# Attention packed into 32 rows and a gated feed-forward: loads of k, q, v and p issued singly behind weight pieces, and the second batch's even sums of v ahead of its odd scores

## The chip, the cores and the metric

The kernel runs on one core of one Trainium2 chip. The metric is the device time of one execution in microseconds. Three runs were timed; a further execution was profiled, and all durations below come from that one.

## What is computed

Eight batches of eight heads attend twice. First 32 packing rows p attend to k and v of 576 rows; then q attends to the packed rows. The result, 4608 tokens of 512, goes through a gated feed-forward without a nonlinearity.

```python
def sm_attn(qq, kk, vv):
    s = scale * np.matmul(qq, kk.transpose(0, 1, 3, 2))
    a = np.exp(s - np.max(s, axis=-1, keepdims=True))
    a = a / (np.sum(a, axis=-1, keepdims=True) + 1e-09)
    return np.matmul(a, vv)
p_packed = sm_attn(p, k, v)
out = sm_attn(q, p_packed, p_packed)
x = out.transpose(0, 2, 1, 3).reshape(B * S, H * D)
return ((x @ w_a) * (x @ w_b)) @ w_out
```

## The kernel before, in words

Every matmul of the feed-forward is made of three: each operand is split into a rounded high part and a low part, and high x high, high x low and low x high are added in PSUM. The tiles hold heads in two halves, "even" and "odd" (e = 0, 1); the loads, the scores and the sums of v are made once for each.

**The work of a batch.** `stage1` (L268) makes the scores of p against k (L276), their maximum, the exponentials (L294), their transposition (L315, L316), and the sums of v (L325), which VectorE scales into `pp` (L331). `stage2` (L334) makes the scores of q against the packed rows (L340) and their softmax into `a2_hi` and `a2_lo`. `g_tiles` (L395) folds the packed rows into the weights w_a and w_b, `mm1` (L416) makes the two gated factors, VectorE multiplies them (L431), and `mm2_part` (L442) multiplies by w_out.

**The order is written by hand.** All five engines run their instructions in the order in which the program issues them. Strings of steps set that order: `START` for the beginning, and `PLAN_0`, one piece between two bars for each slot between the half products of batch 0. In them `S0`/`S1` are the even and odd scores of the next batch, `r0`/`r1` the further steps of the even and odd `stage1` (the fourth one after the scores makes the sums of v), `s0`/`s1` those of `stage2`, `k`, `q` and `T` transpose k, q and p on VectorE (`turn` L120, `turn_p` L245), and `A B C D` convert a piece of the weights. `Lk`, `Lq`, `Lv`, `Lp` load k, q, v and p.

**Loads.** All loads that matter here are issued on SyncE's queue. A weight piece (`raw`, 512 KB, L224 and L231) is loaded as soon as a converted one leaves its buffer (`load_pieces`); 24 of them make w_a and w_b, 12 make w_out. `load` (L107) brings one half of k or q in four DMAs of 144 KB each, in packets of 128 bytes; `load_p` brings p in four of 32 KB, `load_v` a half of v in two of 256 KB and two of 32 KB. Each of these sends its DMAs at once, so that k or q goes out as a burst of four. A DMA also waits until the one eight places ahead of it has landed, because eight semaphores go round. `nat0` and `nat1` take k and then q; `vt` holds one half of v, so that the odd half can be loaded only when the even sums have read the even one.

**Banks.** PSUM tiles come from three pools. `m` has two bank pairs, which the half products of `mm1` and, behind them, the four output tiles of `mm2_part` take in turn (tiles 0 and 2 in one pair, 1 and 3 in the other). `s` is a single bank pair: the scores, the transposed exponentials and the sums of v of a later batch all go through it.

Of the kernel before, what the change touches and what calls it, by code (L numbers as in the profile page):

```python
# [19 lines left out]
def tile_packed_attn_gated_ffn(  # L20
# [20 lines left out]
    nc = tc.nc  # L41
    B, H, S, D = q.shape
    J = p.shape[2]
    DM, DF = w_a.shape
    DO = out.shape[1]
    P = 128
    R, E = 4, 2
# [3 lines left out]
    TL = 32  # L51
    TX = S // TL
    XH = TX // 2
    TR = HS - 2 * P
# [48 lines left out]


    nats, xTs = {}, {}

    def load(src, key, b, i):  # L107


        t = ld.tile([P, R, XH, TL], F32, name=f"nat{i}")  # L110
        rows = src[b, R * i:R * i + R].rearrange("h s d -> (h s) d")
        rows = rows.rearrange("(y l u) d -> u l y d" if key == "k" else "(y u l) d -> u l y d", u=2, l=TL)
        for u in range(2):
            for w in range(2):
                g = 64 * u + 32 * w
                nc.sync.dma_start(
                    out=t[g:g + TL].rearrange("l h x d -> l (h x) d"), in_=rows[u][:, :, TL * w:TL * w + TL])
        nats[key, b, i] = t

    def turn(key, b, i):  # L120
# [43 lines left out]
    def load_v(b, e):  # L164


        t = ld.tile([P, R, NT, D], F32, name="vt") if b or e == 0 else scratch.tile([P, R, NT, D], F32, name="vt1")
        vv = v[b].rearrange("(r e) s d -> e s r d", e=E)[e]
        n = 2 if b else 4
        for i in range(4 // n):  # L170
            nc.sync.dma_start(
                out=t[:, :, n * i:n * i + n, :].rearrange("p r u d -> p r (u d)"),
                in_=vv[n * P * i:n * P * i + n * P].rearrange("(p u) r d -> p r u d", u=n).rearrange("p r u d -> p r (u d)"))
        for u in range(2):
            nc.sync.dma_start(
                out=t[TR * u:TR * u + TR, :, 4, :],
                in_=vv[4 * P:S].rearrange("(p u) r d -> u p r d", u=2)[u])
        vts[b, e] = t

    def load_p(b, queue=None):  # L180
        if b:
            t = sm.tile([P, H, TL], F32, name="p_nat", bufs=1)
            halves = p[b].rearrange("h j (g d) -> g j h d", g=2)
            for g in range(4):
                nc.sync.dma_start(out=t[J * g:J * g + J], in_=halves[g % 2])
        else:
            t = sm.tile([P, 2, 2, D], F32, name="p_nat", bufs=1)
            rows = p[b].rearrange("h j d -> (h j) d").rearrange("(p c) d -> p c d", c=2)
            x = scratch.tile([P, 2, D], F32, name="p_in")
            queue.dma_start(out=x.rearrange("p c d -> p (c d)"), in_=rows.rearrange("p c d -> p (c d)"))  # L190
            nc.vector.tensor_copy(out=t, in_=x.unsqueeze(2).broadcast_to([P, 2, 2, D]))
        p_nat[b] = t
# [36 lines left out]
    def load_wout(f):  # L229
        raw = wop.tile([P, DO, 2], U32, name="raw", tag="w")  # L230
        nc.sync.dma_start(  # L231
            out=raw, in_=w_out.bitcast(U32)[P * f:P * f + P, :].rearrange("p (n t) -> p n t", t=2))
        raws[NC, f] = raw
# [248 lines left out]
    def emit(b, plan, tasks={}):  # L482

        for name in plan.split():
            if name in tasks:
                next(tasks[name], None)
                continue
            if name == "Z":
                warm_first()
                continue  # L490
            if name in "Ww":
                warm(9 if name == "W" else 1)
                continue
            if name in "ABCD":
                convert(name)
                continue
            what, e = name[:-1], int(name[-1])
            n = b + (e // 2 if b or what[0] == "L" else 0)
            if n >= B:
                continue  # L500
            if what == "S":
                if e == 0:
                    st[b] = [stage1(b, 0), stage1(b, 1), stage2(b, 0), stage2(b, 1)]
                next(st[b][e])
            elif what == "s":
                next(st[b][2 + e], None)
            elif what == "r":
                next(st[b][e], None)
            elif what == "T":
                turn_p(n)  # L510
            elif what == "P":
                turned(ppT[:, b % 2:b % 2 + 2], pp.pop(b), b % 2)
            elif what in ("k", "q"):
                turn(what, n, e % 2) if b else turn_first(what, e)
            elif what == "Lk":
                load(k, "k", n, e % 2)
            elif what == "Lq":
                load(q, "q", n, e % 2)
            elif what == "Lv":
                load_v(n, e % 2)  # L520
            elif what == "Lp":
                load_p(n)

    st = {}

# [2 lines left out]
    def warm_first():  # L528

        x = bank_pair()[:, 0, :]  # L530
        nc.tensor.matmul(out=x[:, 0:2 * P], lhsT=zero[:, 0:P], rhs=zero, start=True, stop=True)

    FIRST = ("k0 P0 K1 k2 q0 q1 v0 q2 v1 w1 w1 w1 w1 w1 w1 w1 w1 w1 w1 w1")
    START = ("Z Z Z Z T0 k0 k1 k2 k4 k3 q0 S0 S1 r0 r1 q1 q2 r1 r0 r0 r1 q4 r0 r1 q3 P0 s0 s1 B W A s0 B A A B s0 A s0 C B s1 C s1 s0 B C s1 A s1 B C Lp2 A A B s0 g s1 s0 g w s1 g C B B B C A Lk2 A C A B C A A B B Lk3 C C")
    WAYS = ("000000021020002100012012011200010010")
    TURN = ("1101110010")
    SUBS = ("0000")
# [1 line left out]
    PLAN = (" |  |  | S0 | r0 | r0 |  | r0 |  | r0 Lv1 ; S1 | r1 | r1 q0 Lk2 | r1 | r1 | q1 Lk3 Lv2 P0 |  ; s0 | s0 s0 | s0 T2 | "  # L539
            "s0 Lp4 | s0 s1 | s1 s1 | s1 | s1 | s1 | t0 t1 t2 t3 u0 | k2 |  | k3 Lq2")  # L540
    PLAN = dict(enumerate(PLAN.split("|")))
    PLAN_0 = ("A | C C | B A B A | B C C B C | A A | C | B Lv0 | C B A T0 k0 Lp2 | A A B C Lq0 | C k1 | A B A B A C | S0 B | B A r0 | C C C B A Lq1 | | | C C B r0 r0 D A A | S1 C D | B C B B A D | r1 C | A A D | r0 T2 | | q0 B r1 C B D r1 C | | A D B | C Lv1 A r1 A B D | Lk2 B C B q1 D Lk3 A A P0 | C s0 s0 D C Lp4 A B | s1 s0 | Lv2 | D | s0 s1 s0 | k2 s0 s1 C k3 | s1 | | Lq2 D s0 s1 s1 Lq3 s1")
    PLAN_0 = dict(enumerate(PLAN_0.split("|")))

    pieces = [(c, n) for c in range(NC) for n in range(4)] + [(NC, f) for f in range(NFT)]
    unloaded, to_do = list(pieces), {x: list(pieces) for x in "ABC"}

    def load_pieces(n):

        for _ in range(n):  # L550
            if unloaded and len(raws) + len(wo_hi) + len(wo_f32) < NFT:
                c, r = unloaded.pop(0)
                if c < NC:
                    load_w(c, r)
                else:
                    load_wout(r)

    def convert(x):

        if x == "D":  # L560
            if wo_f32:
                split_wout(wo_f32.pop(0))
                load_pieces(2)
            return
        if not to_do[x]:
            return
        c, n = to_do[x].pop(0)
        if (c, n) not in raws:
            load_pieces(1)
        raw = raws[c, n]  # L570
        if x == "A":
            high_word(raw)
        elif x == "B":
            low_word(raw, int(WAYS[pieces.index((c, n))]))
        else:
            assert len(to_do["A"]) <= len(to_do[x]) and len(to_do["B"]) <= len(to_do[x])
            if c < NC:
                i, rr = divmod(n, 2)
                both_words(w_ab[:, c, 2 * rr:2 * rr + 2, 2 * P * i:2 * P * i + 2 * P], raw)
            else:  # L580
                t = sm.tile([P, DO], F32, name="wo_f32", bufs=1)
                both_words(t, raw)
                wo_f32.append(t)
            del raws[c, n]
            load_pieces(2)

    def warm(n):

        x = bank_pair()[:, 0, :]
        t = firsts["k", 0].rearrange("p h t -> p (h t)")  # L590
        for _ in range(n):
            nc.tensor.matmul(out=x, lhsT=ident, rhs=t[:, 0:512], start=True, stop=True)
# [17 lines left out]
    for name in FIRST.split():  # L610
        what, i = name[0].lower(), int(name[1])
        queue = nc.sync if what == name[0] else nc.scalar
        if what == "p":
            load_p(0, queue)
        elif what == "v":
            load_v(0, i)
        elif what == "w":
            load_pieces(i)
        else:
            load_first(k if what == "k" else q, what, i, queue)  # L620
    tasks = {"g": next_g(0)}
    emit(0, START, tasks)
    drain(tasks["g"])
# [53 lines left out]
    for b in range(NB):  # L677
        plan = dict(PLAN if b else PLAN_0)
        slot, tasks, late_steps = [0], {"g": next_g(b + 1)} if b == 0 else {}, [""]
# [280 lines left out]
    i, c0 = tiles[-1]  # L960
# [35 lines left out]
```

## Time and profile before

| | us |
|---|---|
| median of three runs | 709.51 |
| lowest and highest run | 708.51, 713.61 |
| the profiled execution | 712.88 |
| span of its trace, first to last instruction | 711.1 |
| mean granted TensorE clock, share of full | 0.997 |
| TensorE matmuls busy | 699.6 (98%) |
| VectorE, ScalarE, GpSimd busy | 449.5, 364.7, 410.7 |

Times inside the trace count from the start of the span. The profiled execution lies 3.4 us above the median of the runs. A busy TensorE is not TensorE at its peak, since matmuls overlap and their ends are modelled; what its timeline shows reliably is when it stood and for whom. In a row of a timeline the bracket at the end gives the idle time just before it and what ended it. "SPq" is SyncE's queue, on which a row is the time that the issue of a DMA took, and "DMA" in the chain of waits is a transfer from its issue to its landing.

### The profile page before, as it was taken

How to read it: one execution, taken by the hardware profiler on the slowest of the kernel's cores; microseconds unless marked ns; L12 is line 12 of the kernel's file. 1: busy time of each engine (PE TensorE's matmuls, PEld its weight loads, DVE VectorE, ACT ScalarE, POOL GpSimd, SP SyncE). 2: the span in 40 equal slices, each digit the busy share in tenths (PEclk: the TensorE clock that was granted, in tenths of full speed). 3: DMA queues.
4: the chain of work that ended last, by engine and by line, in shares of the span. 5: the costliest groups of instructions: out<-in, count | busy, mean ns of one | idle time of the engine just before them, and what ended most of it. 6: DMA issues, size and time to landing. Idle time of an engine off the chain costs nothing.

```text
span 711.1 us, 14173 instructions
## 1 busy us (share of the span) xinstructions
PE 699.6 (98%) x5542; PEld 574.8 (81%) x5542; DVE 449.5 (63%) x825; ACT 364.7 (51%) x731; POOL 410.7 (58%) x320
## 2 busy tenths in 40 slices
PE   8999989999999999999999999999999999999998
PEld 6487867888778887887888788788788888888886
DVE  4988645367355669665875678765785667754342
ACT  5988734454344455644563456554555445544510
POOL 0556633337334787745874579566775577856520
PEclk9999999999999999999999999999999999999999
DMA  9999962668344745556444573456246323133002
GB/s 311 378 212 321 244 127 62 184 152 289 90 96 141 217 93 144 136 138 148 136 105 125 143 191 94 108 177 168 72 103 176 105 90 120 60 118 119 1 1 74
DMA packets 180371, 102.57 MB, mean 144 GB/s; under 512 B 145744, under 2 KB 161744, under 8 KB 174928
## 3 DMA queue, kind: packets, MB, share of 16 engines
q1 hardware_dynamic: 179888, 101.08, 50.8%
q8 instruction: 43, 0.70, 0.4%
q10 hardware_dynamic: 416, 0.59, 0.2%
q14 instruction: 24, 0.20, 0.1%
HBM read 85.92 MB, written 15.73 MB: 143 GB/s over the span
## 4 chain that ended last, share of the span: by engine, by line
PE 89%; DMA 7%; DVE 1%; ACT 1%; SPq 1%; issue 1%; DVEq 0%; ACTq 0%
PE x L764 37%; PE m L805 29%; PE m L416 8%; PE x L819 5%; PE m L442 4%; DMA raw<-in_moe_w_a_dram 2%; DMA vt<-in_v_dram 2%; PE s L325 2%; DMA raw<-in_moe_w_out_dram 1%; PE s L340 1%; PE s L276 1%; PE x L395 1%; PE s L315 1%; DMA wr<-w_kept 1%; DMA nat<-in_k_dram 1%
## 5 line engine op out<-in xcount | busy, mean ns | idle before, releaser
L764 PE MATMUL x<-wo,h_hi 128*128 128x512 f32 (+1 forms) x776 | 249.3, 391 | 0.3 <-ACT gs L825 0.3
L91 POOL TENSOR_TENSOR h_lo<-asb,h_hi 128x576 fp32r<-128x576 f32 x96 | 140.0, 1460 | 89.2 <-ACT h_hi L435 45.1
L764 PEld LDWEIGHTS x<-wo,h_hi 128*128 128x128 f32 x776 | 140.8, 188 | 22.4 <-ACT gs L825 1.3
L764 PE MATMUL x<-wo,h_lo 128*128 128x512 f32 (+1 forms) x388 | 152.0, 392 | 0.0
L91 POOL TENSOR_TENSOR G_lo<-gs,G_hi 128x640 fp32r<-128x640 f32 x72 | 112.9, 1573 | 30.9 <-ACT G_hi L840 30.6
L764 PEld LDWEIGHTS x<-wo,h_lo 128*128 128x128 f32 x388 | 72.9, 188 | 11.7
L91 POOL TENSOR_TENSOR A_lo<-gs,A_hi 128x256 fp32r<-128x256 f32 x36 | 27.2, 755 | 89.3 <-ACT A_hi L828 89.3
L887 DVE TENSOR_TENSOR d<-m,d 128x576 f32<-128x576 f32 (+1 forms) x73 | 54.1, 741 | 34.9 <-ACT d L883 34.1
L900 DVE TENSOR_TENSOR asb<-m,d 128x288 f32<-128x288 f32 x72 | 32.5, 451 | 64.1 <-ACT c L896 60.7
L896 ACT COPY c<-m 128x288 f32<-128x288 f32 x72 | 28.7, 399 | 83.2 <-PE m L805 83.2
L774 DVE TENSOR_TENSOR part<-x,part 128x512 f32<-128x512 f32 (+1 forms) x65 | 44.1, 678 | 38.7 <-PE x L764 38.7
L805 PE MATMUL m<-tx_hi,G_hi 128*128 128x288 f32 x216 | 63.8, 295 | 0.0
L805 PE MATMUL m<-tx_hi,G_lo 128*128 128x288 f32 x216 | 63.7, 295 | 0.0
L825 ACT COPY gs<-x 128x512 f32<-128x512 f32 x36 | 21.1, 587 | 83.0 <-PE x L819 81.4
L805 PE MATMUL m<-tx_lo,G_hi 128*128 128x288 f32 x216 | 63.3, 293 | 0.0
L840 ACT CAST G_hi<-gs 128x640 fp32r<-128x640 f32 x72 | 52.2, 729 | 15.1 <-POOL gs L834 14.5
L883 ACT COPY d<-m 128x576 f32<-128x576 f32 (+1 forms) x73 | 46.7, 639 | 20.1 <-PE m L805 18.5
L850 ACT CAST h_hi<-asb 128x576 fp32r<-128x576 f32 x72 | 49.0, 680 | 11.5 <-DVE asb L914 11.5
L805 PEld LDWEIGHTS m<-a_hi,G_hi 128*128 128x128 f32 x144 | 27.0, 187 | 31.8 <-issue 17.4
L834 POOL TENSOR_TENSOR gs<-gs 128x512 f32<-128x512 f32 x36 | 46.6, 1295 | 2.6 <-DVE gs L831 2.5
L805 PE MATMUL m<-a_hi,G_hi 128*128 128x288 f32 x144 | 46.6, 324 | 0.0
L913 DVE TENSOR_TENSOR m<-m,c 128x288 f32<-128x288 f32 x72 | 33.3, 463 | 17.7 <-PE m L805 16.0
(168 smaller groups left out, 1553.5 us busy)
## 6 DMA issues: line engine op xcount, KB each, us to landing
wr<-w_kept SPq DMA_DIRECT2D x36, 1024.0 KB, 5.1
nat<-in_k_dram SPq DMA_DIRECT2D x56, 144.0 KB, 5.3
nat<-in_q_dram SPq DMA_DIRECT2D x56, 144.0 KB, 5.3
vt<-in_v_dram SPq DMA_DIRECT2D x28, 256.0 KB, 3.6
out_dram<-part SPq DMA_DIRECT2D x27, 256.0 KB, 2.0
raw<-in_moe_w_a_dram SPq DMA_DIRECT2D x12, 512.0 KB, 8.4
raw<-in_moe_w_b_dram SPq DMA_DIRECT2D x12, 512.0 KB, 9.6
raw<-in_moe_w_out_dram SPq DMA_DIRECT2D x12, 512.0 KB, 6.9
```

The source lines that it names most:

```text
L91: return eng.tensor_tensor(out=dst, in0=src, in1=hi.bitcast(F32), op=ALU.subtract)
L416: nc.tensor.matmul(out=ps[:, half, 0:HS], lhsT=gt[:, kt, ft % 4, cols], rhs=at[:, kt, HS * half:HS * half + HS], start=(n == 0 and kt == 0 ...
L764: nc.tensor.matmul(out=o[:, cols], lhsT=ht[:, c0:c0 + P], rhs=wt[:, cols], start=(ft == fts[0] and n == 0), stop=end)
L774: nc.vector.tensor_tensor(out=parts[i][:, cols], in0=o[:, cols], in1=parts[i][:, cols], op=ALU.add)
L805: nc.tensor.matmul(out=bank[:, n % 2, 0:HS], lhsT=g, rhs=t, start=(first and i == 0), stop=(i == 2), skip_group_check=True)
L819: nc.tensor.matmul(out=gps[e][J * r:J * r + J, :], lhsT=ppT[rows, 2 * (b % 2), r, :], rhs=w[rows, r, :], start=True, stop=True)
L834: nc.gpsimd.tensor_tensor(out=gs[:, 2:4].rearrange("p a u f -> p a (u f)"), in0=gs[:, 0:2].rearrange("p a u f -> p a (u f)"), in1=s2.unsqu ...
L840: nc.scalar.copy(out=G_hi[:, n % 3], in_=gs[:, 1:6, n % 2])
L850: nc.scalar.copy(out=view(h_hi[ft]), in_=src)
L883: nc.scalar.copy(out=d[:, both], in_=X[:, both, 0:HS])
L887: nc.vector.tensor_tensor(out=d[:, both], in0=V[:, both, 0:HS], in1=d[:, both], op=ALU.add)
L913: nc.vector.tensor_tensor(out=v, in0=v, in1=c2, op=ALU.add)
```

## The change

Loads are no longer sent where they are asked for. `load`, `load_v` and `load_p` put their DMAs into a list, `parcels`, with a size, and `send` takes them from its front: after each weight piece as many as fit into 144 (a k or q piece counts 72, a p piece 16, half a v 32), and all of them once no weight piece is left to load. With the last weight piece loaded, each load is sent at once, as before.

```diff
+    parcels, unloaded = [], []
+    def parcel(size, out, in_):
+        parcels.append((size, out, in_))
+    def send(room=None):
+        while parcels and (room is None or parcels[0][0] <= room):
+            size, out, in_ = parcels.pop(0)
+            nc.sync.dma_start(out=out, in_=in_)
+            room = room and room - size
...
-                nc.sync.dma_start(
-                    out=t[g:g + TL].rearrange("l h x d -> l (h x) d"), in_=rows[u][:, :, TL * w:TL * w + TL])
+                parcel(2 * XH * R, t[g:g + TL].rearrange("l h x d -> l (h x) d"), rows[u][:, :, TL * w:TL * w + TL])
...
-                nc.sync.dma_start(out=t[J * g:J * g + J], in_=halves[g % 2])
+                parcel(2 * H, t[J * g:J * g + J], halves[g % 2])
...
+            if what[0] == "L" and not unloaded:
+                send()
...
+    ROOM = 144
...
                     load_wout(r)
+                send(ROOM)
+                if not unloaded:
+                    send()
...
         elif what == "v":
             load_v(0, i)
+            send()
```

Of the strings of steps, `START` asks for both halves of k of batch 1 directly behind `Lp2` instead of later. In `PLAN_0` the second half of q (`Lq1`) moves from slot 13 to slot 9, p of batch 2 (`Lp2`) from slot 7 to slot 11, the even sums of v (the last `r0`) from slot 21 to slot 17, ahead of `S1`, and the odd half of v (`Lv1`) from slot 26 to slot 17 behind them. `T2`, which transposes p of batch 2, stays in slot 21.

```diff
-    ... | S0 B | B A r0 | C C C B A Lq1 | | | C C B r0 r0 D A A | S1 C D | ... | r0 T2 | ... | C Lv1 A r1 A B D | ...
+    ... | S0 B Lp2 | B A r0 | C C C B A | | | C C B r0 r0 D A A | r0 Lv1 S1 C D | ... | T2 | ... | C A r1 A B D | ...
```

On SyncE's queue, from the last weight pieces of w_out on, the order before is this. `nat` with q is q of batch 1, the first `vt` its even half of v and the second its odd half, `p_nat` is p of batch 2.

```order
L171 DMA vt<-in_v_dram 128x4x128 x2
L175 DMA vt<-in_v_dram 32x4x64 x2
L231 DMA raw<-in_moe_w_out_dram 128x1024
L185 DMA p_nat<-in_p_dram 32x8x32 x4
L231 DMA raw<-in_moe_w_out_dram 128x1024
L116 DMA nat_731<-in_q_dram 32x36x32 x4
L231 DMA raw<-in_moe_w_out_dram 128x1024 x5
L116 DMA nat_874<-in_q_dram 32x36x32 x4
L231 DMA raw<-in_moe_w_out_dram 128x1024
L171 DMA vt<-in_v_dram 128x4x128 x2
L175 DMA vt<-in_v_dram 32x4x64 x2
```

The same place of SyncE's queue now (the lines of the changed kernel stand 9 to 17 further down; L116 is the `send` of all parcels, L240 the w_out piece):

```order
L116 DMA vt<-in_v_dram 128x4x128 x2
L116 DMA vt<-in_v_dram 32x4x64 x2
L240 DMA raw<-in_moe_w_out_dram 128x1024 x2
L116 DMA nat_726<-in_q_dram 32x36x32 x2
L240 DMA raw<-in_moe_w_out_dram 128x1024
L116 DMA nat_726<-in_q_dram 32x36x32 x2
L240 DMA raw<-in_moe_w_out_dram 128x1024
L116 DMA nat_750<-in_q_dram 32x36x32 x2
L240 DMA raw<-in_moe_w_out_dram 128x1024
L116 DMA nat_750<-in_q_dram 32x36x32 x2
L240 DMA raw<-in_moe_w_out_dram 128x1024
L116 DMA p_nat<-in_p_dram 32x8x32 x4
```

The q pieces stand in pairs between weight pieces, and p of batch 2 has moved from ahead of all q to behind it, directly ahead of the last weight piece and the odd half of v. One w_out piece more stands ahead of the even half of v. The k pieces of batch 1, further up, are taken apart in the same way, with one piece of w_a more ahead of their end.

On TensorE, at the odd scores of batch 1 (`xT` is transposed k, `pT` transposed p), before:

```order
L416 MATMUL m<-a_hi,glo 128x288 x4
L276 MATMUL s<-xT_703,pT 32x288 x2
L276 MATMUL s<-xT_755,pT 32x288 x2
L276 MATMUL s<-xT_703,pT 32x256 x2
L276 MATMUL s<-xT_755,pT 32x256 x2
```

And now:

```order
L425 MATMUL m<-a_hi,glo 128x288 x4
L334 MATMUL s<-vt,t_947 32x64 x20
L285 MATMUL s<-xT_703,pT 32x288 x2
L285 MATMUL s<-xT_748,pT 32x288 x2
L285 MATMUL s<-xT_703,pT 32x256 x2
```

The even sums of v, which stood 27 rows further down, now stand directly ahead of the odd scores; both write the bank pair `s`.

On VectorE, from the reciprocal of the even row sums to the transposition of p of batch 2 (`pT<-p_nat`), before:

```order
L301 RECIPROCAL rs<-rs 128x1
L431 TENSOR_TENSOR asb<-m,asb 128x576
L214 SCALAR_TENSOR_TENSOR wo_f_990<-raw 128x512
...
L431 TENSOR_TENSOR asb<-m,asb 128x576
L331 TENSOR_SCALAR pp<-s,rs 128x64 x2
L249 STREAM_TRANSPOSE pT<-p_nat 128x256
L431 TENSOR_TENSOR asb<-m,asb 128x576
```

And now:

```order
L310 RECIPROCAL rs<-rs 128x1
L440 TENSOR_TENSOR asb<-m,asb 128x576
L340 TENSOR_SCALAR pp<-s,rs 128x64 x2
L223 SCALAR_TENSOR_TENSOR wo_f_1019<-raw 128x512
...
L440 TENSOR_TENSOR asb<-m,asb 128x576
L258 STREAM_TRANSPOSE pT<-p_nat 128x256
L440 TENSOR_TENSOR asb<-m,asb 128x576
```

The scaling of the even sums has moved up behind one product; the transposition of p stands where it stood, between the last two products of `mm1` of batch 0.

## Rows read from the trace of the kernel before

**Rows 1.** Stretches of 20 us: length, busy of each engine, PEclk, DMA share, GB/s.
```profile
80.00:100.00 20.00, 17.46 (x117) 13.53 (x119) 8.75 (x14) 10.56 (x19) 8.43 (x7) 0.91 0.90 162
100.00:120.00 20.00, 20.00 (x140) 14.72 (x139) 11.84 (x18) 6.26 (x12) 9.30 (x8) 1.00 0.25 62
```

**Rows 2.** Chain of waits around the odd sums: start us, us, what.
```profile
86.63 5.64 DMA vt<-in_v_dram
...
92.76 4.29 PE m L442 x12
...
97.27 2.75 PE m L442 x12
```

**Rows 3.** Timeline of TensorE: start us, us, work [idle before <-releaser].
```profile
53.60 0.71 PE L276 MATMUL s<-xT,pT 64*32 64x288 f32 x20 [0.28 <-DVE xT L124]
...
56.39 0.53 PE L416 MATMUL m<-a_hi,ghi 128*128 128x288 f32 x2 [0.28 <-DVE asb L431]
...
63.65 0.53 PE L416 MATMUL m<-a_hi,ghi 128*128 128x288 f32 x2 [0.98 <-ACT asb L428]
...
75.87 0.90 PE L325 MATMUL s<-vt,t 128*32 128x64 f32 x40
...
90.26 0.43 PE L325 MATMUL s<-vt,t 128*32 128x64 f32 x16 [1.34 <-DMA vt<-in_v_dram]
```

**Rows 4.** Timeline of SyncE's queue, the second burst of q.
```profile
74.99 9.36 SPq L116 DMA_DIRECT2D nat<-in_q_dram  x4
```

**Rows 5.** Stretches during and after bursts; 57 to 62 weights alone, 97 to 100 k and p.
```profile
39.00:42.00 3.00, 3.00 (x31) 2.00 (x30) 3.00 (x4) 2.77 (x5) 2.12 (x2) 1.00 0.45 65
57.00:62.00 5.00, 5.00 (x47) 4.00 (x46) 4.29 (x7) 4.82 (x10) 3.45 (x2) 1.00 1.04 411
66.00:69.00 3.00, 3.00 (x53) 2.06 (x51) 2.53 (x5) 3.00 (x7) 2.33 (x2) 1.00 0.64 127
72.00:75.00 3.00, 3.00 (x25) 3.00 (x24) 2.75 (x5) 2.39 (x5) 2.83 (x3) 1.00 0.84 172
83.00:85.00 2.00, 2.00 (x11) 1.65 (x10) 0.80 (x1) 1.11 (x3) 0.66 (x2) 1.00 0.59 91
97.00:100.00 3.00, 3.00 (x23) 2.23 (x25) 1.02 (x2) 1.64 (x3) 0.94 (x1) 1.00 1.07 169
```

**Rows 6.** Last q piece, then last even v: issue ns min/median/max, starts, time to landing.
```profile
L116 SPq DMA_DIRECT2D nat<-in_q_dram x1: 1278/1278/1278, 83.1 to 83.1; - x1
...
DMA to landing us min/median/max: 3.5/3.5/3.5
...
L175 SPq DMA_DIRECT2D vt<-in_v_dram x2: 507/2188/3870, 57.1 to 61.0; - x2
...
DMA to landing us min/median/max: 6.2/8.1/9.9
```

**Rows 7.** A microsecond in which q runs beside a weight piece.
```profile
81.00:82.00 1.00, 1.00 (x6) 0.79 (x5) 1.00 (x2) 0.93 (x2) 0.18 (x1) 1.00 1.39 139
```

**Rows 8.** Stretches of 2 us at the odd sums.
```profile
90.00:92.00 2.00, 0.80 (x32) 0.57 (x32) 0.00 (x0) 0.59 (x2) 1.27 (x1) 1.00 1.11 142
92.00:94.00 2.00, 1.74 (x17) 1.32 (x12) 1.17 (x4) 0.25 (x1) 0.00 (x0) 0.54 0.94 147
```

**Rows 9.** Timelines of TensorE and VectorE at the odd scores and first output tiles.
```profile
67.58 0.69 PE L276 MATMUL s<-xT,pT 64*32 64x288 f32 x20
...
81.25 0.62 PE L442 MATMUL m<-wo,h_hi 128*128 128x512 f32 x2
...
67.76 0.76 DVE L431 TENSOR_TENSOR asb<-m,asb 128x576 f32<-128x576 f32 x1 [0.17 <-PE m L416]
...
78.08 0.46 DVE L331 TENSOR_SCALAR pp<-s,rs 128x64 f32<-128x64 f32 x2
78.46 0.43 DVE L249 STREAM_TRANSPOSE pT<-p_nat 128x256 f32<-128x256 f32 x1
80.28 0.76 DVE L431 TENSOR_TENSOR asb<-m,asb 128x576 f32<-128x576 f32 x1 [1.39 <-PE m L416]
```

More of the change, by code (lines that the diff above doesn't have):

```diff
@@ L170, in load_v @@
         for i in range(4 // n):
-            nc.sync.dma_start(
-                out=t[:, :, n * i:n * i + n, :].rearrange("p r u d -> p r (u d)"),
-                in_=vv[n * P * i:n * P * i + n * P].rearrange("(p u) r d -> p r u d", u=n).rearrange("p r u d -> p r (u d)"))
+            parcel(
+                8 * R, t[:, :, n * i:n * i + n, :].rearrange("p r u d -> p r (u d)"),
+                vv[n * P * i:n * P * i + n * P].rearrange("(p u) r d -> p r u d", u=n).rearrange("p r u d -> p r (u d)"))
         for u in range(2):
-            nc.sync.dma_start(
-                out=t[TR * u:TR * u + TR, :, 4, :],
-                in_=vv[4 * P:S].rearrange("(p u) r d -> u p r d", u=2)[u])
+            parcel(2 * R, t[TR * u:TR * u + TR, :, 4, :], vv[4 * P:S].rearrange("(p u) r d -> u p r d", u=2)[u])
         vts[b, e] = t
@@ L533, in tile_packed_attn_gated_ffn @@
     FIRST = ("k0 P0 K1 k2 q0 q1 v0 q2 v1 w1 w1 w1 w1 w1 w1 w1 w1 w1 w1 w1")
-    START = ("Z Z Z Z T0 k0 k1 k2 k4 k3 q0 S0 S1 r0 r1 q1 q2 r1 r0 r0 r1 q4 r0 r1 q3 P0 s0 s1 B W A s0 B A A B s0 A s0 C B s1 C s1 s0 B C s1 A s1 B C Lp2 A A B s0 g s1 s0 g w s1 g C B B B C A Lk2 A C A B C A A B B Lk3 C C")
+    START = ("Z Z Z Z T0 k0 k1 k2 k4 k3 q0 S0 S1 r0 r1 q1 q2 r1 r0 r0 r1 q4 r0 r1 q3 P0 s0 s1 B W A s0 B A A B s0 A s0 C B s1 C s1 s0 B C s1 A s1 B C Lp2 Lk2 Lk3 A A B s0 g s1 s0 g w s1 g C B B B C A A C A B C A A B B C C")
+    ROOM = 144
     WAYS = ("000000021020002100012012011200010010")
@@ L541, in tile_packed_attn_gated_ffn @@
     PLAN = dict(enumerate(PLAN.split("|")))
-    PLAN_0 = ("A | C C | B A B A | B C C B C | A A | C | B Lv0 | C B A T0 k0 Lp2 | A A B C Lq0 | C k1 | A B A B A C | S0 B | B A r0 | C C C B A Lq1 | | | C C B r0 r0 D A A | S1 C D | B C B B A D | r1 C | A A D | r0 T2 | | q0 B r1 C B D r1 C | | A D B | C Lv1 A r1 A B D | Lk2 B C B q1 D Lk3 A A P0 | C s0 s0 D C Lp4 A B | s1 s0 | Lv2 | D | s0 s1 s0 | k2 s0 s1 C k3 | s1 | | Lq2 D s0 s1 s1 Lq3 s1")
+    PLAN_0 = ("A | C C | B A B A | B C C B C | A A | C | B Lv0 | C B A T0 k0 | A A B C Lq0 | C k1 Lq1 | A B A B A C | S0 B Lp2 | B A r0 | C C C B A | | | C C B r0 r0 D A A | r0 Lv1 S1 C D | B C B B A D | r1 C | A A D | T2 | | q0 B r1 C B D r1 C | | A D B | C A r1 A B D | Lk2 B C B q1 D Lk3 A A P0 | C s0 s0 D C Lp4 A B | s1 s0 | Lv2 | D | s0 s1 s0 | k2 s0 s1 C k3 | s1 | | Lq2 D s0 s1 s1 Lq3 s1")
     PLAN_0 = dict(enumerate(PLAN_0.split("|")))
     pieces = [(c, n) for c in range(NC) for n in range(4)] + [(NC, f) for f in range(NFT)]
-    unloaded, to_do = list(pieces), {x: list(pieces) for x in "ABC"}
+    unloaded.extend(pieces)
+    to_do = {x: list(pieces) for x in "ABC"}
     def load_pieces(n):
```

## The prediction

> **What bounds the kernel now.** I read the stretches of 20 us first, then the chain of waits, then the timelines of TensorE, of SyncE's queue and of VectorE around each wait. In the stretches TensorE is full from 100 us on, while in 80 to 100 us it misses 2.5 us and its granted clock is 0.91; beside it the reader is to see the DMA share, 0.90 up to 100 us and 0.25 after [rows 1]. The loads of weights and of batch 1 are one backlog that is worked off soon after 100 us, and only up to there can an order of loads matter.
>
> The chain of waits crosses one transfer of that backlog: the second half of v of batch 1 lands at 92.27 (86.63 + 5.64), the odd sums end at 92.76, and then twelve output matmuls take 4.29 us where the next twelve take 2.75 [rows 2]. TensorE's timeline shows four places to win. It waits 0.28 us for the transposed k, 0.28 for a product of VectorE, 0.98 for a copy of ScalarE, and at the odd sums it has nothing from 88.92 on (90.26 - 1.34); the same forty matmuls of the even sums took 0.90 [rows 3]. I put the first three down to late data too: the k by its releaser, the other two because the product and the copy stand in their engines' order behind conversions of weight pieces.
>
> SyncE's queue shows why data is late. The burst of four q pieces that starts at 74.99 holds the queue for 9.36 us [rows 4], and the weight piece and v behind it are issued that much later. During and just after such bursts the DMA engines run partly empty: a share of 0.45 in 39 to 42, 0.64 in 66 to 69, 0.84 in 72 to 75 and 0.59 in 83 to 85, against 1.04 with weights alone [rows 5].
>
> **The change part by part.** No instruction is added on any engine, and the bytes are the same. Three things move: the k and q pieces in between weight pieces, the load of p of batch 2 behind all of q, and the even sums of v ahead of the odd scores.
>
> *The stream.* Up to the last q piece both orders carry the same transfers, so I ask when the last of them lands. Before, it was issued at 83.1 and took 3.5 us: 86.6 [rows 6]. The empty shares, measured against 1.05, are 3 x 0.60 + 3 x 0.41 + 3 x 0.21 + 2 x 0.46 = 4.6 us [rows 5]; if all is filled, it lands at 82.0. Then the pieces themselves. At the 169 GB/s of a stretch of k and p alone 144 KB take 0.87 us; at the weights' 411 GB/s they would take 0.36 [rows 5]; those are the ends. In a moment when q runs beside weights the share is 1.39 [rows 7], against 1.07 without them, so more is in flight at once: 0.87 x 1.07 / 1.39 = 0.67. I take that, since the new order makes such moments the rule, and sixteen pieces save 16 x 0.20 = 3.2 us. I let a fifth of the empty time (0.9) remain, as the pieces still come in pairs. The last transfer ahead of the final weight piece, now p of batch 2, lands at 82.0 - 3.2 + 0.9 = 79.7. Bounds: 73.8 (all filled, 0.36 a piece) and 86.6 (nothing gained).
>
> The Trainium skill (DMA: Bandwidth & Descriptors, "Why small descriptors are slow") gives every packet a fixed 3 cycles beside one per 32 bytes. Packets of 128 bytes would then cost 7/4 of the weights' time, an estimate of 0.63 us a piece; the trace's 0.87 without weights speaks against it, the 0.67 is close. By that rule p would land 0.6 us earlier and the sum below would be 0.6 us lower.
>
> *The three small waits.* k of batch 1 has one weight piece more ahead of its end now (512 KB at 411 GB/s: 1.3 us), against the 1.8 us of emptiness in 39 to 42 and 8 x 0.20 of its own pieces, about 2 us in its favour; the weights behind it have no piece more ahead of them. All three waits are shorter than that, so I take them whole, -1.54; bounds 0 and -1.54.
>
> *The odd sums.* Before, the last of v landed 5.7 us behind the last q (92.3 and 86.6); with the same weight piece between them that gives 85.4 now. TensorE comes to them at 88.92 less what it has gained by then, about 88.6. The wait goes with 3 us to spare: 92.76 - 88.92 - 0.90 = 2.94, so -2.94. Bounds -2.94 and 0. What is late next is q for the scores after them, which lands ahead of p.
>
> *The clock.* After the odd sums TensorE's granted clock was 0.54 of full in 92 to 94, between its two levels (1.2 and 2.4 GHz) and near the lower, when it had been busy for 0.80 of the 2 us before [rows 8]. Without the gap: 4.29 - 2.75 = -1.54; bounds -1.54 and 0 (a new gap takes its place).
>
> *The even sums.* They now stand directly ahead of the odd scores, and both write the only bank pair s. So the scores wait until VectorE has scaled the sums into pp, and the scaling stands behind a product there. In the clock of before TensorE would end the sums at 67.58 + 0.90 = 68.48, VectorE the product at 68.52 and the two scalings (0.46) at 68.98 [rows 9]: +0.50, with all of TensorE's next matmuls behind it. Bounds 0 and 1.0 (twice as late). Their v has one more weight piece ahead of it, 1.3 us. It landed at 67.2 before (61.0 + 6.2) [rows 6]; the same 1.8 and 1.6 as above bring it to 65.1, and TensorE asks at 67.58 - 1.54 = 66.0.
>
> *The p of batch 2.* VectorE transposed it at 78.46, then sat 1.39 us until TensorE was done, then multiplied the product that frees the second bank pair m, and the second output tile starts there at 81.25 [rows 9]. The transposition keeps its place, but p now lands at 79.7. With 0.43 + 0.76 behind it and a handover the bank is free at 80.9, and TensorE is there at 81.25 - 1.54 + 0.50 = 80.2: +0.7. Bounds: 0 if p lands before 79.0, +3.0 at 82.0.
>
> Sum: -1.54 - 2.94 - 1.54 + 0.50 + 0.70 = -4.8 us. The profiled execution took 712.9 us, 711.1 of them the span; it becomes 708.1. The median of the runs shown, 709.5, lies 3.4 lower, and the same sum makes it 704.7, my forecast.
>
> **Rivals.**
>
> *Nothing is filled (slower).* The 128-byte pieces may hold the engines wherever they stand: the share of 1.07 without weights speaks for it, the 0.45 and 0.59 around bursts against. Then p lands at 86.6, VectorE frees the bank at 87.8, and TensorE, which stood there at 81.25, loses 6.5 us, the even sums' 0.5 included. It gains none of the small waits; it still gains 2.94, since it comes to the odd sums after v; the slow clock moves to the new gap. 6.5 - 2.9 = +3.6, so 713.1. The sign turns when p lands after 84.5, or after 83.0 where the gap brings the slow clock with it.
>
> *The gap moves and takes the clock along.* The empty time is filled but the pieces stay at 0.87: p at 82.0, a wait of 3.0 us at the second output tile, slow matmuls behind it. -1.54 - 2.94 + 0.50 + 3.0 = -1.0, so 708.5. For it speaks the only rate of pieces that a row shows without weights; against it, the share of 1.39 beside them.
>
> *Everything is hidden.* Pieces near the rate of weights and p before 79.0: -5.5, so 704.0. The share of 1.39 speaks for it, the still paired pieces against.
>
> **How the numbers follow.** Forecast 0.58, the gap with the clock 0.18, everything hidden 0.14, nothing filled 0.10. The range of 702.6 to 709.2 holds the first three, with the spread of a median whose runs lay between 708.5 and 713.6, and leaves the slower rival out. A difference of 1%, 7.1 us, is about what a measurement of this kernel can tell from no change. The waits in reach make 6.0 us together, so faster by over 1% would need luck in the runs: 0.06. Slower by over 1% would need the slower rival and as much again: 0.04. Within 1%: 0.90.
>
> **What would show it.** Right: a DMA share near 1.0 or above from 39 to 80 us; no wait at the odd sums and no clock under 1.00 in 92 to 96; half a microsecond of TensorE waiting for VectorE's scaling ahead of the odd scores; the transposition of p waiting 2 to 4 us on VectorE. Wrong: over 2 us of waiting at the second output tile, even sums that wait for v, odd sums that still wait, or empty DMA stretches as before.

## The result, and the profile after

The changed kernel takes 719.15 us (median of 6 runs, 718.35 to 720.84), the kernel before, timed beside it, 709.07 (6 runs, 707.91 to 713.61). The ratio is 1.0133, with a 95% interval of 1.0104 to 1.0163. The forecast was 704.7, within 1%; the time lies above its range.

The profiled execution of the changed kernel took 718.4 us, its span 716.6. In the stretches of 20 us the loss stands where the prediction looked for the gain; this row answers to the first of [rows 1], in the same columns:

```profile
80.00:100.00 20.00, 14.32 (x97) 11.41 (x97) 6.08 (x11) 8.15 (x15) 7.82 (x6) 0.83 0.67 154
```

TensorE was busy for 17.46 us between 80 and 100 before, and for 14.32 now, and its granted clock over this stretch fell from 0.91 to 0.83. TensorE's timeline shows the places, answering to [rows 3] (start us, us, work, and in brackets the idle time before it and what ended it):

```profile
52.10 0.53 PE L425 MATMUL m<-a_hi,ghi 128*128 128x288 f32 x2 [0.67 <-DVE asb L440]
...
55.63 0.72 PE L285 MATMUL s<-xT,pT 64*32 64x288 f32 x20 [1.06 <-DVE xT L135]
...
69.83 0.69 PE L285 MATMUL s<-xT,pT 64*32 64x288 f32 x17 [0.68 <-DVE pp L340]
...
88.61 1.22 PE L451 MATMUL m<-wo,h_hi 128*128 128x512 f32 x2 [5.68 <-DVE asb L440]
...
98.48 0.90 PE L334 MATMUL s<-vt,t 128*32 128x64 f32 x40
```

The odd sums (98.48) no longer wait. In their place TensorE waits 5.68 us at the second output tile. The chain of waits says for what, and answers to [rows 2] (start us, us, what); the row of VectorE's timeline below it answers to the transposition in [rows 9]:

```profile
84.89 2.45 DMA p_nat<-in_p_dram
...
87.46 0.06 DVE pT L258
...
87.83 0.73 DVE asb L440
...
88.61 9.95 PE m L451 x33
98.55 0.83 PE s L334 x40
99.38 2.95 PE m L451 x12
```

```profile
79.03 0.74 DVE L440 TENSOR_TENSOR asb<-m,asb 128x576 f32<-128x576 f32 x1
87.46 0.45 DVE L258 STREAM_TRANSPOSE pT<-p_nat 128x256 f32<-128x256 f32 x1 [7.69 <-DMA p_nat<-in_p_dram]
```

The p of batch 2 lands at 87.34 (84.89 + 2.45). VectorE has stood at its transposition since 79.77, and the product that frees the second bank pair m is queued behind it. The first of the 33 matmuls that follow are the slow ones: the pair at 88.61 takes 1.22 us, where the same pair took 0.62 before [rows 9]. In the rows for the stretches the granted clock (third number from the end), which answers to [rows 8], is 0.50 there, the lower of its two levels (1.2 GHz of 2.4), after 5.6 us without a matmul:

```profile
83.00:88.60 5.60, 0.00 (x0) 0.00 (x0) 1.14 (x3) 0.01 (x1) 0.00 (x0) 0.81 0.77 202
88.60:92.60 4.00, 4.00 (x9) 3.15 (x10) 2.67 (x4) 3.01 (x7) 1.93 (x2) 0.50 0.98 221
92.60:96.00 3.40, 3.40 (x15) 2.79 (x14) 1.03 (x2) 2.50 (x6) 1.94 (x2) 0.90 0.56 89
```

The stretches that were half empty before [rows 5] show where the stream went (same columns; the last number is GB/s, ahead of it the DMA share):

```profile
39.00:42.00 3.00, 3.00 (x33) 2.00 (x31) 3.00 (x5) 2.98 (x6) 2.42 (x2) 1.00 0.98 235
42.00:45.00 3.00, 3.00 (x26) 3.00 (x24) 2.38 (x5) 2.25 (x5) 1.44 (x1) 1.00 0.78 149
...
57.00:62.00 5.00, 5.00 (x45) 3.84 (x44) 4.13 (x8) 4.32 (x8) 3.11 (x2) 1.00 1.03 410
66.00:69.00 3.00, 2.98 (x58) 2.67 (x56) 2.89 (x5) 2.83 (x6) 2.66 (x2) 1.00 1.05 338
69.00:72.00 3.00, 2.32 (x51) 1.21 (x44) 1.16 (x4) 1.78 (x4) 2.46 (x3) 1.00 0.63 95
...
75.00:78.00 3.00, 3.00 (x24) 2.96 (x23) 2.38 (x4) 2.71 (x6) 2.13 (x2) 1.00 0.98 235
```

39 to 42 and 66 to 69 are full now, as predicted. But 42 to 45 and 69 to 72 are partly empty (0.78 and 0.63), and where k or q is on its way beside weights (39 to 42, 75 to 78) the share is near 1 while only 235 GB/s move, against 410 with weights alone. The empty time has moved by some microseconds, and what is full is slow.

SyncE's queue tells the same; [rows 4] had 9.36 us for one burst:

```profile
67.70 3.61 SPq L240 DMA_DIRECT2D raw<-in_moe_w_out_dram  x1
71.36 2.61 SPq L116 DMA_DIRECT2D nat<-in_q_dram  x2
74.08 0.80 SPq L240 DMA_DIRECT2D raw<-in_moe_w_out_dram  x1
...
79.98 2.16 SPq L240 DMA_DIRECT2D raw<-in_moe_w_out_dram  x1
82.19 3.15 SPq L116 DMA_DIRECT2D p_nat<-in_p_dram  x4
```

The weight pieces with a q pair between them land at 75.48, 78.92, 82.35 and 86.31 (start of the issue and time to landing in the trace): 3.61 us a group on average. Weight pieces that run alone land 1.34 us apart (54.41, 55.75 and 57.10 in the trace of before); less that, 1.13 us are left for each q piece, and the queue now stands at weight pieces where it stood at the third piece of a burst. The last q lands at 83.8 instead of 86.6 [rows 6], 2.0 of these 2.8 us because p (0.7) and one weight piece (1.34) now come behind q and not ahead.

### The profile page after: what moved, and what is told of

It is laid out like the page before. It is cut to its first block, busy times and chain, and to the rows that moved or that the text cites. A ratio compares the mean times of both kernels' runs of the same rounds, so it can differ in the third digit from the quotient of the medians.

```text
span 716.6 us, 14168 instructions
## 1 busy us (share of the span) xinstructions
PE 700.8 (98%) x5542; PEld 575.0 (80%) x5542; DVE 449.2 (63%) x825; ACT 364.6 (51%) x731; POOL 410.8 (57%) x320
## 4 chain that ended last, share of the span: by engine, by line
PE 90%; DMA 4%; DVE 2%; SPq 1%; ACT 1%; issue 1%; POOL 1%; DVEq 0%; ACTq 0%; POOLq 0%
PE x L781 37%; PE m L822 29%; PE m L425 8%; PE m L451 5%; PE x L836 5%; DMA raw<-in_moe_w_b_dram 2%; PE s L334 2%; PE s L349 1%; DMA vt<-in_v_dram 1%; PE s L285 1%; PE x L404 1%; PE s L324 1%; DMA nat<-in_k_dram 1%; DVE xT L135 0%; SPq L116 0%
```

## The experiments

Theory 1: a k or q piece costs the stream about 1.1 us wherever it stands, and p of batch 2, moved behind all of q, is what costs the time. Rival: sending pieces singly costs by itself. Then: why is a piece so dear? The short diffs are against the kernel named; parts of the two slot tables that don't change are left out.

**p ahead of q again**, in the changed kernel:

```diff
-C B A T0 k0 |   S0 B Lp2 |
+C B A T0 k0 Lp2 |   S0 B |
```

> The changed kernel with one part undone: p of batch 2 is again loaded ahead of q (its place before the change); single sending and the moved even sums stay. Theory 1 (p behind all of q is what costs): the transposition of p on VectorE waits under 0.5 us, the second output tile no longer waits 5.68 us, its 33 matmuls no longer take 9.95 us but about 7.7; TensorE is then at the odd sums at about 90.6 and waits some 0.5 to 1 us for v (which lands near 91.4 as in the changed kernel). Time 718.4 - 5.7 - 2.3 + 0.5 to 1.5 = 711 to 712. Rival (sending single pieces costs by itself, because weights and k come later): at most 2 us come back, 716 or more. Third (p is the cause and the stream is faster without it): 708 or less.

Measured 712.23 us (10 runs), 1.0022 of before (1.0002 to 1.0043). TensorE's timeline:

```profile
56.20 1.03 PE L285 MATMUL s<-xT,pT 64*32 64x288 f32 x20 [1.70 <-DVE xT L135]
...
71.84 0.69 PE L285 MATMUL s<-xT,pT 64*32 64x288 f32 x17 [0.92 <-DVE pp L340]
...
92.36 0.90 PE L334 MATMUL s<-vt,t 128*32 128x64 f32 x40
```

The big wait is gone and with it five sixths of the loss (1.0133 to 1.0022). TensorE waits 1.70 us for k, and the last of v lands at 92.36, just as it comes to the odd sums.

**p behind q alone**, in the kernel before:

```diff
-C B A T0 k0 Lp2 |   C C C B A Lq1 |
+C B A T0 k0 |   C C C B A Lq1 Lp2 |
```

> The kernel before with one part alone: p of batch 2 moved behind the last q burst, bursts and sums as they were. Theory 1: p lands at 87 (q ended at 86.6 before), VectorE transposes it near 87.3, the second output tile waits from 81.3 to 88.4, about 7 us, slow matmuls follow it, and the wait of 2.9 us at the odd sums goes: 709 + 7 - 2.9 + up to 1 = 713 to 714, ratio to before about 1.006. Rival (the interleaving is what costs): no change, within 0.2% of before.

Measured 716.74 us, 1.0105 (1.0074 to 1.0136). VectorE's and TensorE's timelines:

```profile
85.97 0.45 DVE L249 STREAM_TRANSPOSE pT<-p_nat 128x256 f32<-128x256 f32 x1 [8.37 <-DMA p_nat<-in_p_dram]
```

```profile
87.11 1.22 PE L442 MATMUL m<-wo,h_hi 128*128 128x512 f32 x2 [6.61 <-DVE asb L431]
```

One edit, with all bursts as they were, makes four fifths of the loss. I had expected 1.006, taking off the wait at the odd sums and adding up to 1 us of slow clock. The slow clock took 2.1: TensorE needs 9.66 us from 87.11 to the odd sums at 96.77, where it needed 7.60 at the full clock with p ahead of q (84.76 to 92.36). The rest suggests that before has less of that wait than its profile shows.

**The kernel before once more**, for that reason:

> The kernel before, unchanged, profiled in another execution. Its first profile is of 712.9 us, its median is 709.1. If the odd sums' wait of 2.9 us and the slow clock behind it belong to every execution, they show again, v landing 5 to 6 us behind the last q, and the 3.8 us lie elsewhere; if they are what made that execution long, the wait is under 1 us and the time 708 to 710.

It took 708.49 us, its span 706.7:

```profile
63.37 0.54 PE L416 MATMUL m<-a_hi,ghi 128*128 128x288 f32 x2 [1.43 <-ACT asb L428]
...
88.67 1.12 PE L325 MATMUL s<-vt,t 128*32 128x64 f32 x40
```

There is hardly a wait at the odd sums: the last of v landed at 89.42, while they ran (1.12 us instead of 0.90), where it landed at 92.28 in the first profile. Of the 54 runs of before that stand beside these experiments, 17 had a granted clock of 0.998 or less over the span; 16 of these took over 711 us, against 2 of the other 37. I take the wait with its slow clock to be a thing of about a third of the executions; the profiled one, 712.88 us at 0.997, was of this third.

**Single sending alone** (the changed kernel with p and the even sums at their places of before):

```diff
-C B A T0 k0 |   S0 B Lp2 |   r0 Lv1 S1 C D |   T2 |      C A r1 A B D
+C B A T0 k0 Lp2 |   S0 B |   S1 C D |          r0 T2 |   C Lv1 A r1 A B D
```

> The changed kernel with p of batch 2 and the even sums where they stood before: single sending alone. Theory 1 (a piece costs the stream the same 1.1 us wherever it stands): last q lands within 1 us of before's 86.6, v at 91 to 92, the odd sums wait 1 to 3 us as before, k waits about 1 us on TensorE instead of 0.28; no wait over 1 us at the second output tile. Time within 0.3% of before (707 to 711). Rival (single sending costs by itself): 714 or more. By my forecast (stream faster by some us): 705 or less.

Measured 712.15 us (10 runs), 1.0037 (1.0019 to 1.0055):

```profile
56.84 0.72 PE L285 MATMUL s<-xT,pT 64*32 64x288 f32 x20 [2.09 <-DVE xT L135]
...
92.29 0.43 PE L334 MATMUL s<-vt,t 128*32 128x64 f32 x16 [1.50 <-DMA vt<-in_v_dram]
```

It is slightly slower than before, and not faster; the time lies between what theory 1 (707 to 711) and the rival (714 or more) had said, so single sending does cost something by itself. k and v come later, not earlier: the last of k lands at 55.29 (52.05 before), the last of v at 93.73 (92.28 and 89.42 in the two profiles of before).

**The moved even sums alone**, in the kernel before:

```diff
-S1 C D |          r0 T2 |   C Lv1 A r1 A B D
+r0 Lv1 S1 C D |   T2 |      C A r1 A B D
```

> The kernel before with one part alone: the even sums of v ahead of the odd scores, with the request for the odd half of v that follows them; bursts and p as before. The order of the loads on SyncE's queue does not change by it, so v lands as before, 89 to 93. Theory 1: a wait of 0.5 to 0.9 us ahead of the odd scores for VectorE's scaling of the sums, part of which comes back at the odd sums where these wait for v: ratio 1.000 to 1.001. Rival (the moved sums are what takes the odd sums' wait away): 0.996 to 0.998.

Measured 709.08 us (10 runs), 0.9980 (0.9965 to 0.9994), with before at 710.25 beside it: a little faster (0.2%), which is the rival. None of its ten runs had a granted clock under 0.999, against 5 of 12 of before.

```profile
69.19 0.69 PE L276 MATMUL s<-xT,pT 64*32 64x288 f32 x17 [0.69 <-DVE pp L331]
...
89.73 0.90 PE L325 MATMUL s<-vt,t 128*32 128x64 f32 x40
```

The 0.69 us for the bank pair s is there. TensorE then reaches the odd sums at 89.73 instead of 88.67, while v comes as ever (90.25 here). I read it as a short wait that keeps a longer one, and the slow clock behind it, from happening; no run tests this by itself.

**k in bursts, q singly, p first, sums moved:** the eight k pieces go back to their bursts (the condition in the last line sends p and v at once too).

```diff
-B C Lp2 Lk2 Lk3 A A B ... C A A C A B C A A B B C C
+B C Lp2 A A B ... C A Lk2 A C A B C A A B B Lk3 C C
-if what[0] == "L" and not unloaded:
+if what[0] == "L" and (not unloaded or what != "Lq"):
```

> As the kernel with p of batch 2 first, but the eight k pieces of batch 1 go out in two bursts of four at their old places; q still goes out singly and the even sums stay ahead. Theory 1 (what single sending costs by itself is the later k, 54.7 against 51 to 52): k lands by 52.5, TensorE waits for the transposed k under 0.5 us instead of 1.70, the wait for the bank pair s (0.7 to 0.9) stays; 1 to 1.5 us come back, ratio to before 0.999 to 1.002. Rival (the single q pieces or the sums cost it): as before that edit, 1.002 or more.

Measured 712.87 us (4 runs), 1.0053 (1.0034 to 1.0071); a miss. k is better by half (the wait for it is 0.79 us), and the time goes elsewhere:

```profile
91.04 0.43 PE L334 MATMUL s<-vt,t 128*32 128x64 f32 x16 [1.23 <-ACT wo L248]
92.10 1.05 PE L334 MATMUL s<-vt,t 128*32 128x64 f32 x24 [0.62 <-DMA vt<-in_v_dram]
```

TensorE comes to the odd sums at 89.8, and v, behind the single q pieces, lands at 92.66. The first row names a copy of ScalarE that the sums don't read; it ends as the first piece of v lands (90.91), so I take both waits to be for v. In these three kernels, then, single sending costs at k, at v or at both, and what it costs is small (0.2 to 0.5%).

**The transposition of p two instructions later on VectorE**, with the changed kernel's loads:

```diff
-T2 |  |   q0 B r1 C B D r1 C
+ |  |     q0 T2 B r1 C B D r1 C
```

> The changed kernel with its loads as they are; only the transposition of p of batch 2 stands two instructions later on VectorE, behind the product that frees the bank of the second output tile and behind the next transposition of q. Theory 1 (the late p costs only because VectorE's order puts that product behind it): p still lands near 87, VectorE still waits for it, but the second output tile does not wait; time as with p ahead of q, 711 to 713, ratio to before 1.001 to 1.005. Rival (the bank waits for late data in any order): 716 or more.

Measured 713.49 us (10 runs), 1.0036 (1.0016 to 1.0057). VectorE's timeline:

```profile
81.84 0.76 DVE L440 TENSOR_TENSOR asb<-m,asb 128x576 f32<-128x576 f32 x1 [2.03 <-PE m L425]
82.51 1.37 DVE L135 STREAM_TRANSPOSE xT<-nat 128x1152 f32<-128x1152 f32 x1
87.38 0.45 DVE L258 STREAM_TRANSPOSE pT<-p_nat 128x256 f32<-128x256 f32 x1 [3.50 <-DMA p_nat<-in_p_dram]
```

p is as late as ever, and the second output tile starts at 82.81 without a wait. The 5.68 us are a matter of what stands behind the transposition on its engine. TensorE now loses 1.28 us at 98.95, to a later copy of VectorE (`ppT`, L273), which stands behind another transposition there.

**Why a piece is dear.** Four kernels change only how the k and q pieces of batches 1 and later are cut: packets of 256 bytes (whole rows of half the tiles) into 32 partitions; packets of 4608 bytes into 32 partitions; packets of 128 bytes in two transfers into all 128 partitions; packets of 4608 bytes in one transfer into all 128. They put the numbers of k and q in other places, so their results are not those of the reference, and only their times are read.

```diff
-parcel(2 * XH * R, t[g:g + TL]..., rows[u][:, :, TL * w:TL * w + TL])
+parcel(2 * XH * R, t[g:g + TL]..., rows[u][:, 18 * w:18 * w + 18, :])
```

> The changed kernel with packets of 256 bytes instead of 128 in the pieces of k and q of batches 1 and later: a piece takes whole rows of 64 numbers of half the tiles, instead of half rows of all; same bytes, half the packets, so the scores are of other data. Theory A (a piece's price is per packet, about 1.15 us for 1152 packets wherever it stands): a group of one weight piece and two k or q pieces takes about 2.5 instead of 3.6 us, the last q lands 6 to 9 us earlier, p with it ahead of 80, the wait of 5.68 us at the second output tile is under 1 us, time 707 to 711. Rival B (the price comes from SyncE's queue standing still between issues): groups still take 3.3 us or more, p lands after 84, time 715 or more.

```diff
+flat = src[b, R * i:R * i + R]...rearrange("(g l f) -> g l f", g=4, l=TL)
-parcel(2 * XH * R, t[g:g + TL]..., rows[u][:, :, TL * w:TL * w + TL])
+parcel(2 * XH * R, t[g:g + TL]..., flat[2 * u + w])
```

> The changed kernel with the pieces of k and q of batches 1 and later read as contiguous rows of 4608 bytes for each partition: same bytes, 32 rows a piece instead of 1152, so the scores are of other data. Theory A (price per packet): a piece costs the weights' rate, about 0.4 us, a group 2.1 us, and the last q lands 10 to 13 us earlier, unless free buffers for weights bound the stream first; no wait at the second output tile, time 706 to 710. Rival B (the queue): groups 3.3 us or more, time 715 or more.

```diff
+rows = src[b, R * i:R * i + R]...rearrange("(y l) d -> l y d", l=P)
+for w in range(2):
+    parcel(4 * XH * R, t[:, 2 * w:2 * w + 2]..., rows[:, :, TL * w:TL * w + TL])
```

> The changed kernel with packets of 128 bytes as it has them (half rows), but a half of k or q is two transfers of 288 KB into all 128 partitions instead of four of 144 KB into 32; one such transfer goes behind a weight piece where two pieces went (the scores are of other data). Theory P (at 128 bytes the packet is the price, 13.2 ns each on an engine, whatever the partitions): 2304 packets still take 144 x 13.2 ns = 1.9 us of each engine, a group stays at 3.2 us or more, p of batch 2 lands at 84 to 88, the second output tile waits 3 us or more, 715 to 719. Theory C (32 partitions are the price at any packet size): a transfer takes about 0.8 us, a group 2.1 to 2.6, p lands ahead of 80, no wait over 1 us there, 706 to 710.

```diff
+flat = src[b, R * i:R * i + R]...rearrange("(l f) -> l f", l=P)
+parcel(2 * XH * R, t..., flat)
```

> The kernel with packets of 4608 bytes once more, but a half of k or q is one transfer of 576 KB into all 128 partitions instead of four of 144 KB into 32 partitions each: the same packets, the same bytes, and one of them behind each weight piece (the scores are of other data). Theory C (a piece is dear because it writes into 32 partitions only): the 576 KB cost about 1.5 us of the stream, as 512 KB of weights cost 1.3, and the weights beside them stay at 1.3; the second half of q lands near 73 to 76, p behind it ahead of 79, no wait at the second output tile, 706 to 710. Rival D (reads of k and q are slow into any partitions): 576 KB cost 3 us or more as in the kernel with four pieces, q lands near 82 and the second output tile waits 3 us or more.

One execution each: 719.69, 717.77, 717.21 and 706.88 us. The row of VectorE at the transposition of p is enough to read them by, in this order:

```profile
89.68 0.45 DVE L258 STREAM_TRANSPOSE pT<-p_nat 128x256 f32<-128x256 f32 x1 [9.06 <-DMA p_nat<-in_p_dram]
```

```profile
84.33 0.45 DVE L259 STREAM_TRANSPOSE pT<-p_nat 128x256 f32<-128x256 f32 x1 [6.30 <-DMA p_nat<-in_p_dram]
```

```profile
86.65 0.45 DVE L258 STREAM_TRANSPOSE pT<-p_nat 128x256 f32<-128x256 f32 x1 [7.65 <-DMA p_nat<-in_p_dram]
```

```profile
77.17 0.43 DVE L256 STREAM_TRANSPOSE pT<-p_nat 128x256 f32<-128x256 f32 x1
```

Longer packets alone don't help, and theory A falls; B's times came out, but not by its reason, since SyncE issued most transfers of the 4608-byte kernel in 0.3 to 0.5 us and the groups still took 3.3. More partitions alone don't help either, as theory P had it. With both together the late p is gone, as theory C had it for long packets: q lands at 67.8, p at 70.3, and TensorE waits for neither. Of the 17 us by which p lands earlier, some 2.7 are of two weight pieces fewer ahead of it; and k and q go out in four transfers here instead of sixteen, which no kernel tests by itself. The DMA queues' part of the page says it in one row each, for 40 to 86 us of the changed kernel, of 256, of 4608 bytes, and of 128 bytes into 128 partitions, and for 40 to 76 us of the last (packets, MB, share of 16 engines):

```profile
q1 hardware_dynamic: 23116, 12.26, 97.3%
```

```profile
q1 hardware_dynamic: 13637, 11.67, 113.3%
```

```profile
q1 hardware_dynamic: 7729, 12.86, 102.4%
```

```profile
q1 hardware_dynamic: 22651, 12.42, 100.6%
```

```profile
q1 hardware_dynamic: 7579, 12.48, 98.4%
```

In the first four the engines are full by their share for 46 us over some 12 MB, with 23,116 packets or with 7,729. The fifth moves as much in 36 us.

**A slightly faster version.** In the kernel before, v is what some executions wait for, and the second half of q is needed last. So the odd half of v goes ahead of that half of q, behind the even sums that free its buffer; nothing else moves:

```diff
-C C C B A Lq1 |   r0 T2 |           C Lv1 A r1 A B D
+C C C B A |       r0 Lv1 Lq1 T2 |   C A r1 A B D
```

> The kernel before with its bursts and with p and the even sums at their old places; only the odd half of v of batch 1 is loaded ahead of the second half of q (behind the even sums that free its buffer), where before it came behind. If the late v is what some executions of before lose 1 to 4 us by, v lands at 84 to 87, no execution waits at the odd sums, the slow clock behind them goes, and the second q half lands near 91 and is in time: median 706 to 708, ratio 0.995 to 0.998, and the spread of the runs is smaller than before's 707 to 713. Rival (q then comes late to VectorE, or the 1 to 4 us lie elsewhere): 0.999 to 1.003.

Measured 708.53 us (12 runs, 707.38 to 711.11), with before at 709.53 (23 runs, 707.78 to 714.17): 0.9975 (0.9955 to 0.9995); the ratio is as expected, the median 0.5 us above, and the gain of a quarter of a percent is near the edge of what the runs can tell. TensorE's timeline and SyncE's queue:

```profile
89.08 0.90 PE L325 MATMUL s<-vt,t 128*32 128x64 f32 x40
```

```profile
77.06 0.95 SPq L171 DMA_DIRECT2D vt<-in_v_dram  x2
...
80.62 6.51 SPq L116 DMA_DIRECT2D nat<-in_q_dram  x4
```

v lands at 86.75, with 2.3 us to spare. One of its 12 runs had a granted clock of 0.998 or less, against 7 of 23 of before.

## Why the prediction was wrong

**The stream** is the step that failed. It took 0.67 us for a k or q piece, between 0.87 alone and 0.36 at the weights' rate, and read the empty stretches as time that singly sent pieces would fill. Measured were 1.13 us a piece, above the upper end, and p of batch 2 at 87.3 where 79.7 was forecast, beyond the bound of 86.6 too: 16 x (1.13 - 0.67) = 7.4 of these 7.6 us. The bursts of before cost the same: two weight pieces and four k pieces landed there in 7.31 us (41.49 to 48.80), which less 2 x 1.34 is 1.16 a piece, the empty time in it included. The 0.67 came from one microsecond with a share of 1.39 [rows 7]. A share above 1 there was no more work done; the same row moved only 139 GB/s, at which 144 KB take 1.06 us. The bytes of that row, and not its share, would have come near the price. Of the 4.6 us of empty time little came back: the queue moved 12.26 MB between 40 and 86 us, against 11.79 before, which at 410 GB/s is 1.1 us.

Full, the engines carry k alone at 139 / 0.883 = 157 GB/s (91.5 to 95 us of the changed kernel), against 410 / 1.03 = 398 for weights: 2.5 times the time for a byte. So the estimate of 0.63 us from the Trainium skill (DMA: Bandwidth & Descriptors, "Why small descriptors are slow") fell too: the rule of the fixed cycles gives 7/4. The estimate left out the 32 bytes of metadata with each DMA operation that the same section names.

**The p of batch 2**: the mechanism was right and stands in the trace as described, transposition, product, bank. Its +0.70 was mis-sized by the stream: with p at 87.34 it is 5.68 us, beyond the upper bound of 3.0, which ended at p at 82.0. The run with the transposition two instructions later shows that this wait hangs on the order on VectorE alone.

**The clock**: nothing of the forecast -1.54 came; what came is what its bound named, a new gap that takes the slow clock along. The 33 matmuls from 88.61 take 9.95 us with the sums' handover; with p first the like stretch (84.76 to 92.36) takes 7.6, so the slow clock costs about 2.3 here.

**The even sums** were right in mechanism and nearly in size: +0.50 forecast, 0.68 measured. Their v was not: it was to land at 65.1 and landed at 68.70, later than before (67.28), while the sums ran (from 68.15, 1.00 us instead of 0.90). It cost little because TensorE was late itself.

**The three small waits** were wrong in sign for k (1.06 us, where 0.28 was to go) and for a product (0.67, at an earlier one); the one at the copy of ScalarE went. The last of k landed at 54.07, where it was to come some 2 us earlier than the 52.05 of before.

**The odd sums**: the wait did go, but for another reason: TensorE comes to them 9.6 us later. v lands at 91.4, hardly earlier than the 92.3 of before, where 85.4 was forecast. And here a second error sits: 2.94 and the 1.54 of slow clock are of the profiled execution, 712.88 us, and the step carried the sum over to the median as if each run had them. By their granted clock, two thirds of the runs don't. From one profiled execution to the other the loss is 5.5 us, against the slower rival's +3.6, and 0.8 of the difference is a longer slow clock (2.3 for 1.54); between the medians it is 10.1.

That adds up, against the second profile of before: 0.67 + 1.06 + 0.68 + 5.68 + 2.3 less the 1.64 us that it waits at the like places is 8.8 of the 9.9 us between the spans; 1.1 stays unassigned. By parts, p alone makes 1.0105, single sending 1.0037, and the moved sums 0.9980; the product is 1.0122, beside 1.0133.

**The rival** *Nothing is filled* named the place and the mechanism rightly, and p at 87.3 lies beyond both of its turning points (83.0 and 84.5), which no run tests. With 713.1 it came 6 us short, chiefly because it took off 2.94 for the odd sums and added nothing for the slow clock. Its chance of 0.10 was far too low. That a share of 1.07 stood against only 169 GB/s with k and p alone was in the rows for it.

## What to carry to other kernels

Price a transfer by the bytes that its stretch moves at a full share, never by a share above 1 or by empty time beside it, and do so in a stretch with the same traffic beside it: 144 KB cost 0.94 us alone (157 GB/s) and 1.13 between weights. Before a load is moved behind others, look up the first instruction that reads it, and then what stands behind that one on its engine: a load with slack can still hold a bank by engine order. A profile is one execution; where a removable wait ends within a microsecond of its cause, take a second profile before taking it off a median.

## What the hardware showed that I had not expected

A k or q piece is dear for two reasons at once, and lifting one changes little: p, at 87.34 in the changed kernel, lands at 84.20 with long packets into 32 partitions, at 86.53 with short ones into 128, and at 89.55 with 256 bytes into 32. Where only k is under way, a 128-byte packet takes 0.883 x 16 x 3.5 us / 3868 = 12.8 ns of an engine, with 32 partitions to a transfer, and 0.748 x 16 x 5 us / 4640 = 12.9 with 128:

```profile
q1 hardware_dynamic: 3868, 0.49, 88.3%
```

```profile
q1 hardware_dynamic: 4640, 0.59, 74.8%
```

At this size the packet is the price, whatever the partitions. With packets of 4608 bytes into 32 partitions a piece still costs 1.0 us (weight pieces with a pair between them land at 73.50, 77.20, 80.68 and 83.34, 3.28 us a group); into all 128 partitions, a weight piece and 576 KB of k take 2.74 us (42.04 to 44.78), with q 3.32 (66.11 to 69.43); less 1.34 and by four that is 0.35 to 0.50 us for as many bytes as a piece has. The Trainium skill (SBUF — State Buffer, "Door 1: The DMA port swizzle") says that DMA bandwidth goes by how many of 16 ports the partitions reach. By its formula 32 consecutive partitions reach 8. The runs with long packets agree in direction: 1.0 us against 0.35 to 0.50 is two to three times, where half the ports would give two, an estimate from that rule. The prediction had not asked for it.
